# Attention stage of a one-core kernel: order of tiles, turns of q, place of the x writes, fillers and chores

## The chip, the cores and the metric

The kernel runs on one core of a Trainium2 chip. The metric is the device time in microseconds (us) of one execution, median over runs. TensorE (PE) multiplies, VectorE (DVE) and ScalarE (ACT) read its results from PSUM, GpSimd (POOL) works on SBUF only, and SyncE (SP) issues most of the transfers (DMA).

## What is computed

An attention block without softmax, and behind it a layer of eight experts with balanced routing:

```python
kv = np.einsum('bhsd,bhse->bhde', k, v)          # 8 batches, 8 heads, 576 rows, 64 wide
out = np.einsum('bhsd,bhde->bhse', q, kv)
rms = np.sqrt(np.mean(out * out, axis=-1, keepdims=True) + 1e-06)
out = out / rms * g_norm
x = out.transpose(0, 2, 1, 3).reshape(4608, 512)
logits = x @ w_gate                               # 8 columns, one for each expert
# every token goes to one expert: pairs in the order of falling logits,
# an expert is closed when it has 4608 / 8 = 576 tokens
out[mask_e] = np.maximum(x[mask_e] @ w1[e], 0.0) @ w2[e]   # 512 -> 1024 -> 512
```

## The kernel before

**Stages.** Attention comes first. x, before g_norm, is written to DRAM (x_dram). Then a search on DVE and PE finds the token list of the first expert (`threshold`, `assign`, `fetch`); its tokens are gathered from x_dram by GpSimd and the experts follow one after the other, the search for the next hidden under them. The change touches attention alone (lines 88 to 565).

**A batch of attention** has two parts. `prepare(b)` (line 367) makes what the tiles of batch b need:
- `sum_kv(r)` (391): the sum over rows of k times v for a pair of heads, four pairs r = 0 to 3, 18 matmuls each, into one PSUM tile `kv_ps`. Even and odd rows land on different partitions; ACT copies the odd ones out (`odd`, 415), DVE adds (`kv`, 417), and two copies on POOL put kv into `kvx` twice, once on each half of the partitions (423).
- `turn_q(n)` (375): four transposes of q blocks through PSUM (two for n = 4), copied to `qt` by DVE for n = 1 and 2, by ACT else. There are five, n = 0 to 4; the first half of q (h = 0) is read by n = 0, 1, 2, the second half by n = 2, 3, 4.
- kv is transposed (`t_ps`, 431), copied by ACT (`kvt`, 433), multiplied with the gate weights (`w_ps`, 442), and DVE puts the result beside kv in `kvx` (444). So a tile gives out and its part of the logits in one matmul of 72 columns.

`qt_ps`, `t_ps`, `w_ps` and fillers without a place of their own share two PSUM buffers (tag `tr`).

`tiles` (453) holds the other part. `one(t, ...)` (464) is one tile of 128 rows: 16 matmuls into `o_ps` (two buffers), then on ACT the squares `sq` (two buffers) and the copy `o_sb`, then on DVE the sums `ms`. An even batch has four tiles. An odd one has a fifth, the short tile: half its rows are the last 64 of the batch before, half the last 64 of its own, so it takes 32 matmuls of half the size and reads `qt` and `kvx` of two batches. `scale` (492) turns ms into 1/rms, one square root on ACT and four steps on DVE; `logits` (500) makes the logits of the batch (`part`, `lg`) on DVE. The scaling of x is done on POOL (511) for batches that end at or before column `last_own` = 31, that is 0 to 6, and for batch 7 by ACT in 40 small steps (516) after all else of attention (`late`).

**Order.** PE, DVE, ACT and SP run their instructions in the order in which the program writes them (`manual_schedule`, 529). `prepare` is a generator: in the loop over batches (533) each tile is followed by one step of `prepare(b + 1)`. Steps: (1) sum 0, turn 0; (2) sum 1, turn 1; (3) sums 2 and 3, odd, kv, kvx; (4) turn 2, t_ps, kvt; (5) turn 3, w_ps, turn 4. In an even batch steps 4 and 5 come without a tile between them.

**Loads.** k, v and q of a batch come in halves (`load`, 82), 576 KB each, two buffers for each name and half, all from SP. `paced` makes each DMA of SP wait until the third one before it has landed. Batches 0 and 1 are asked for at the start, the others two batches ahead, by `again` in `prepare`, in the order k v, k v, q, q.

**Writes.** Two tiles of x make one write (520). After each batch, writes go out while eight or more are waiting (`LAG` = 4), in SP's order, so in between the loads. `xo` has `LAG` + 1 = 5 buffers.

**Fillers.** `ones` (356) are matmuls of 128x512 ones in bf16 that compute nothing that is used: 18 at the start, 5 in the first preparation, two before the sums of each further one, and in each batch one before tile 0 and two before tile 3.

**Chores.** Small pieces of work that are popped from a list: first the constants for the search, then the choice of the best expert for columns 0 to 8, 9 to 17, 18 to 26 (`early`, in batches 2, 4, 6; four pieces each: cap and maximum; `pick`; `code_mx`; `best` and `over_c`). They run after each tile of batches 0 and 1, after tile 3 of each batch, in batch 6 also after tile 2, and after the logits: one, in batch 6 two.

The functions that the change touches, with the profile's line numbers:

## Time and profile before

| what | us |
|---|---|
| median of 3 runs (lowest, highest) | 659.36 (658.04, 663.68) |
| profiled execution | 660.36 |
| its span, first to last instruction | 658.6 |
| attention, first tile to the square root of batch 7 | 18.76 to 122.89 |
| first matmul of the search with all its data | 127.94 |
| first gather of tokens | 155.78 |
| busy over the span: PE, DVE, ACT, POOL | 605.8, 387.8, 194.5, 389.3 |
| mean granted TensorE clock | 0.968 of full |

The profile is of one execution. Its rows give start and duration of instructions by engine, "PEld" being weight loads of TensorE; `L479` is line 479 of the kernel; `[2.98 <-ACT o_sb L486]` says that the engine idled 2.98 us until that instruction let it go on. Busy times of overlapping instructions are longer than the distance of their starts, so distances of starts are used for a step's cost. The granted clock is the share of full speed that TensorE was given.

### The profile page before, as it was taken

What the parts mean: (1) busy time and instruction counts of PE and PEld (TensorE: products, weight loads), DVE (VectorE), ACT (ScalarE), POOL (GpSimd) and SP (SyncE); (2) the same over time, 40 slices, a digit from 0 to 9 for tenths busy, and PEclk for the clock granted to TensorE, in tenths of its full rate; (3) what the DMA queues carried; (4) which work ended last, traced back from release to release, by engine and by line L of the source; (5) the groups of instructions that cost most, each with busy time, mean ns of one, the idle gap of its engine ahead of it and who ended that gap; (6) DMA issues with size and microseconds to landing.
All of it is one profiled execution on the core that took longest, in us unless ns stands there. A gap on an engine that the chain in (4) does not pass through costs nothing.

```text
span 658.6 us, 12759 instructions
## 1 busy us (share of the span) xinstructions
PE 605.8 (92%) x4932; PEld 464.6 (71%) x4932; DVE 387.8 (59%) x1249; ACT 194.5 (30%) x395; POOL 389.3 (59%) x405
## 2 busy tenths in 40 slices
PE   7989998335899999999999999999999999999994
PEld 4767777232678677867786786778678867877873
DVE  4466667778678588668757956976671053123201
ACT  1555665611131223123212222231223123222300
POOL 1035434104585487749846974887388669848822
PEclk9999999657999999999999999999999999999998
DMA  8999989416306402710442072109103620721001
GB/s 270 310 315 295 292 291 340 154 50 199 128 0 204 164 33 71 257 41 33 158 171 73 1 262 99 41 0 323 46 32 100 229 72 1 279 84 37 0 9 64
DMA packets 49852, 91.02 MB, mean 138 GB/s; under 512 B 3712, under 2 KB 20096, under 8 KB 49792
## 3 DMA queue, kind: packets, MB, share of 16 engines
q1 hardware_dynamic: 43200, 71.31, 31.6%
q0 software_dynamic: 5888, 18.88, 8.3%
q8 instruction: 39, 0.64, 0.4%
q14 instruction: 21, 0.17, 0.1%
q10 hardware_dynamic: 704, 0.02, 0.1%
HBM read 71.32 MB, written 18.87 MB: 137 GB/s over the span
## 4 chain that ended last, share of the span: by engine, by line
PE 77%; DVE 9%; DMA 5%; issue 4%; ACT 3%; POOL 1%; POOLq 0%; SPq 0%; DVEq 0%; ACTq 0%
PE x_ps L1065 13%; PE x_ps L1025 11%; PE z_ps L1065 9%; PE y_ps L1065 9%; PE z_ps L1025 7%; PE y_ps L1025 7%; PE o_ps L479 4%; PE y_ps L1127 4%; PE kv_ps L395 3%; PE t_ps L969 3%; PE qt_ps L380 2%; DMA v_sb<-in_v_dram 2%; DMA q_sb<-in_q_dram 2%; PE given_ps L651 1%; PE given_ps L646 1%
## 5 line engine op out<-in xcount | busy, mean ns | idle before, releaser
L1070 ACT COPY h<-x_ps 128x288 f32<-128x288 f32 x93 | 37.2, 400 | 166.5 <-PE x_ps L1065 153.7
L1065 PE MATMUL x_ps<-xs,sw 128*128 128x288 f32 x248 | 71.3, 409 | 0.0
L875 POOL DMA_INDIRECT xg<-x_dram,ids x40 | 38.1, 952 | 51.8 <-DMA w_sb<-in_moe_w_dram 37.7
L992 POOL DMA_INDIRECT out_dram<-y_sb,outs x32 | 31.5, 983 | 55.8 <-DVE y_sb L1163 41.1
L1025 PE MATMUL x_ps<-tw,sh 128*128 128x256 f32 x256 | 61.6, 384 | 0.0
L972 ACT ACTIVATE xt<-t_ps,g_col 128x512 f32<-128x512 f32 (+1 forms) x40 | 25.7, 645 | 110.9 <-PE t_ps L969 110.9
L1065 PEld LDWEIGHTS x_ps<-xs,sw 128*128 128x128 f32 x248 | 46.2, 190 | 14.3 <-issue 1.7
L955 POOL TENSOR_TENSOR sw<-w_sb 128x256 f32<-128x256 f32 x64 | 46.8, 731 | 12.3 <-PE z_ps L1065 9.6
L1017 POOL TENSOR_TENSOR sh<-hid 128x512 f32<-128x512 f32 x32 | 40.7, 1272 | 19.9 <-ACT hid L1040 19.9
L1025 PEld LDWEIGHTS x_ps<-tw,sh 128*128 128x128 f32 x256 | 46.9, 190 | 7.1 <-issue 0.8
L1040 ACT ACTIVATE hid<-hid 128x576 f32<-128x576 f32 x64 | 43.8, 686 | 22.9 <-DVE hid L1079 13.1
L511 POOL TENSOR_TENSOR xo<-o_sb,inv 128x512 f32<-128x512 f32 x31 | 32.9, 1090 | 29.7 <-DVE inv L498 16.6
L1103 POOL TENSOR_TENSOR tw<-w_sb 128x512 f32<-128x512 f32 x32 | 40.1, 1276 | 5.0 <-DMA w_sb<-in_moe_w_dram 5.0
L479 PEld LDWEIGHTS o_ps<-kvx,qt 64*128 64x128 f32 (+1 forms) x640 | 33.7, 181 | 12.0 <-issue 7.1
L479 PE MATMUL o_ps<-kvx,qt 64*128 64x72 f32 (+1 forms) x640 | 38.9, 274 | 3.4 <-ACT o_sb L486 3.4
L1065 PE MATMUL z_ps<-xt,sw 128*128 128x288 f32 x128 | 37.8, 413 | 0.1
L1065 PE MATMUL z_ps<-xs,sw 128*128 128x288 f32 x128 | 37.0, 409 | 0.0
L1065 PE MATMUL x_ps<-xt,w_sb 128*128 128x288 f32 x124 | 36.8, 414 | 0.1
L1065 PE MATMUL y_ps<-xt,w_sb 128*128 128x288 f32 x128 | 36.9, 409 | 0.0
L1065 PE MATMUL y_ps<-xs,w_sb 128*128 128x288 f32 x128 | 36.7, 408 | 0.0
L490 DVE TENSOR_REDUCE ms<-sq 128x8 f32<-128x512 f32 x36 | 24.3, 683 | 20.1 <-ACT sq L485 19.8
L423 POOL COPY kvx<-kv 64x512 f32<-64x512 f32 x16 | 9.7, 607 | 43.9 <-DVE kv L417 26.9
(278 smaller groups left out, 1332.4 us busy)
## 6 DMA issues: line engine op xcount, KB each, us to landing
w_sb<-in_moe_w_dram SPq DMA_DIRECT2D x32, 512.0 KB, 5.7
w_sb<-in_moe_w_dram SPq DMA_DIRECT2D x8, 2048.0 KB, 14.3
k_sb<-in_k_dram SPq DMA_DIRECT2D x16, 576.0 KB, 5.8
v_sb<-in_v_dram SPq DMA_DIRECT2D x16, 576.0 KB, 5.8
q_sb<-in_q_dram SPq DMA_DIRECT2D x16, 576.0 KB, 6.1
x_dram<-xo SPq DMA_DIRECT2D x16, 512.0 KB, 4.4
x_dram<-xo SPq DMA_DIRECT2D x4, 256.0 KB, 4.0
xg<-x_dram,ids POOLq DMA_INDIRECT x40, 5.4
```

The lines of the kernel that those rows point to most:

```text
L479: nc.tensor.matmul(o_ps[rows_at, rp, (2 * r2 + l) * W:(2 * r2 + l + 1) * W], lhsT=turned_q[bn][ks, l, block // 2:block // 2 + m].rearrange ...
L511: nc.gpsimd.tensor_tensor(xo[:, t], o_sb[:, t, :, 0:D], inv[:, t * H:(t + 1) * H].rearrange("p (h o) -> p h o", o=1).to_broadcast([P, H, D ...
L875: tokens = nc.gpsimd.indirect_dma_start(out=xg[0:nr], out_offset=None, in_=x_dram, in_offset=bass.IndirectOffsetOnAxis(ap=ids[0:nr, n:n + ...
L955: in_order(nc.gpsimd.tensor_tensor(o, x, y, op=op))
L992: put = nc.gpsimd.indirect_dma_start(out=out, out_offset=bass.IndirectOffsetOnAxis(ap=ids_of[t][0:nr, n:n + 1], axis=0), in_=y_sb[0:nr, :] ...
L1017: in_order(nc.gpsimd.tensor_tensor(o[:, ms], x[:, ms], y[:, ms], op=op))
L1025: nc.tensor.matmul(p_ps[:, n], lhsT=left[:, f, n * P:(n + 1) * P], rhs=right[:, f], start=first, stop=(f == FH - 1), skip_group_check=True)
L1040: nc.scalar.activation(both, both, ACT.Relu)
L1065: nc.tensor.matmul(p_ps, lhsT=lhs[:, r], rhs=rhs[:, r], start=(m in (1, 2, 4, 5) and r == 0), stop=(r == 1), skip_group_check=(m in (6, 7, ...
L1070: nc.scalar.copy(u, p_ps)
L1103: in_order(nc.gpsimd.tensor_tensor(o, x, y, op=AL.subtract))
L1127: nc.tensor.matmul(y_ps[l * nr:(l + 1) * nr], lhsT=hid[:, l * FH + f, a:a + nr], rhs=w2[:, l * FH + f, :], start=(f == 0), stop=(f == FH - 1))
```

## The change

- The loads of batch 1 come in the order k v k v q q.
- `prepare` has four steps: (1) sums 0 and 1; (2) sums 2 and 3, odd, kv, kvx, turn 0; (3) t_ps, kvt, turns 1 and 2; (4) turn 3, w_ps, turn 4. In the first preparation the turns come at 0 | 1 | 2 | 3 | 4, one place earlier. The next loads are asked for in the same steps: k v, k v, q, q.
- In odd batches the short tile comes first. `qt` and `kvx` have two buffers, not three; `xo` has six.
- Fillers: one before the first and the fourth tile of batches 0 to 2 alone; the two before the sums of each preparation stay; in the first preparation 2, 6 and 5; three before t_ps in the last.
- x of batches 0 to 4 is written after batch 4, when SP has all loads behind it, that of batch 5 after batch 5, the rest at the end. `last_own` is 27, so x of batch 6 too is scaled by ACT at the end.
- Chores come after each tile of batches 0, 1 and 6, after the second and fourth tile of the others, and after the logits of batches 0 to 3.

```diff
-    for b in range(2):
-        for h in range(2):
-            for name in "kvq":
-                load(name, b, h)
+    for b, order in enumerate(("kvqkvq", "kvkvqq")):
+        for n, name in enumerate(order):
+            load(name, b, int(name in order[:n]))
...
-        qt = att.tile([P, 2, NT, HP], FT, name="qt", tag="qt", bufs=3)
+        qt = att.tile([P, 2, NT, HP], FT, name="qt", tag="qt", bufs=2)
...
+        turns = [[0], [1], [2], [3], [4]] if b == 0 else [[], [0], [1, 2], [3], [4]]
+
+        def turn_some():
+            for n in turns.pop(0):
+                turn_q(n)
+                if n in (2, 4):
+                    again("q", n // 2 - 1)
+
         if b > 0:
             ones(2, kv_ps[:, 0, :])
-        for r in range(2):
-            sum_kv(r)
-            if r:
-                again("kv", 0)
-            turn_q(r)
-            yield
+        sum_kv(0)
+        sum_kv(1)
+        again("kv", 0)
+        if b == 0:
+            ones(2)
+        turn_some()
+        yield
+        if b == 0:
+            ones(6)
         sum_kv(2)
         sum_kv(3)
         again("kv", 1)
...
-        kvx = att.tile([P, H, W], FT, name="kvx", tag="kvx", bufs=3)
+        kvx = att.tile([P, H, W], FT, name="kvx", tag="kvx", bufs=2)
         for n in range(2):
             nc.gpsimd.tensor_copy(kvx[n * D:(n + 1) * D, :, 0:D], kv.rearrange("p r l d -> p (r l) d"))
+        turn_some()
         if b == 0:
             ones(5)
         yield
-        turn_q(2)
-        again("q", 0)
+        if b + 1 == B:
+            ones(3)
...
         nc.scalar.copy(kvt, t_ps)
+        turn_some()
         yield
-        turn_q(3)
+        turn_some()
...
-        turn_q(4)
-        again("q", 1)
+        turn_some()
...
-    last_own = GC - (R + 1) // 2
+    last_own = GC - R
...
-        xo = att.tile([P, T, H, D], FT, name="xo", tag="xo", bufs=LAG + 1)
+        xo = att.tile([P, T, H, D], FT, name="xo", tag="xo", bufs=HELD)
...
-            if own or t != T - 2:
+            if not wait:
...
-            for t in range(len(rows)):
-                one(t, copies, {0: 1, 3: 2}.get(t, 0))
+            order = range(len(rows)) if b % 2 == 0 else [len(rows) - 1] + list(range(len(rows) - 1))
+            for n, t in enumerate(order):
+                one(t, copies, 1 if b < 3 and n in (0, 3) else 0, b + 1 == B and n == len(rows) - 2)
                 next(parts, None)
-                if b < 2 or t == 3 or b == 6 and t == 2:
+                if b < 2 or b == 6 or n in (1, 3):
                     chore()
...
-            if b < B - 1:
-                chore(2 if b == 6 else 1)
-
-            while len(writes) >= 2 * LAG:
+            if b < 4:
+                chore()
+
+            while b in (B - 4, B - 3) and writes:
                 writes.pop(0)()
```

More of the change, by code (lines that the diff above doesn't have):

```diff
@@ L445, in prepare @@
         kv_of[b] = kvx
-        turn_q(4)
-        again("q", 1)
-    LAG = 4
+        turn_some()
+    HELD = 6
     writes, late = [], []
-    last_own = GC - (R + 1) // 2
+    last_own = GC - R
     def tiles(c0, rows):
@@ L462, in tiles, with one @@
         own = c0 + T <= last_own
-        def one(t, copies, fill):
+        def one(t, copies, fill, wait):
             o_ps = psa.tile([P, 2, 512], FT, name="o_ps", tag="o", bufs=2)
```

## The prediction

> **What bounds the kernel now.** I read the windows first, cut where TensorE (PE) starts the first tile of a batch. The columns are busy time of PE, weight loads, VectorE (DVE), ScalarE (ACT), GpSimd (POOL), then granted clock, DMA share and GB/s.

> ```profile
> 31.62:46.49 14.87, 12.81 (x286) 10.17 (x285) 9.58 (x42) 8.16 (x16) 5.39 (x6) 1.00 0.95 310
> 59.17:72.23 13.06, 12.65 (x285) 10.07 (x283) 8.84 (x18) 8.16 (x16) 5.40 (x6) 1.00 0.89 282
> 72.23:84.92 12.69, 12.06 (x254) 9.49 (x251) 8.85 (x18) 7.14 (x14) 6.68 (x7) 1.00 0.93 321
> 97.97:111.66 13.69, 12.13 (x253) 9.49 (x251) 10.15 (x21) 7.14 (x14) 6.58 (x7) 1.00 0.87 326
> 111.66:122.89 11.23, 6.26 (x101) 5.04 (x99) 8.66 (x15) 5.92 (x12) 4.25 (x4) 0.81 0.80 300
> ```

> See that batches 3 and 4 (second and third row) are full of PE work, that batches 1 and 6 are longer with the same work, and that batch 7 (last row) is not bound by PE. The PE waits of the whole attention stage say what the rest is:

> ```profile
> PE o_ps L479 <- ACT o_sb L486: 3.4, 2, 3.0
> PE qt_ps L380 <- DMA q_sb<-in_q_dram: 2.6, 2, 1.7
> PE qt_ps L380 <- ACT kvt L433: 2.1, 4, 0.5
> PE qt_ps L380 <- DVE kvx L444: 1.2, 3, 0.4
> ```

> Two waits for q (1.65 in batch 1, 0.94 in batch 6) and one of 3.0 us in batch 7. The timeline shows where that one starts:

> ```profile
> 115.96 2.22 DVE L335 TENSOR_TENSOR over_c<-mx,cand 128x192 bf16<-128x192 f32 x2
> 118.10 2.08 DVE L490 TENSOR_REDUCE ms<-sq 128x8 f32<-128x512 f32 x3
> 118.87 0.60 ACT L485 ACTIVATE sq<-o_ps 128x512 f32<-128x512 f32 x1 [3.51 <-DVE ms L490]
> 120.05 1.24 PE L479 MATMUL o_ps<-kvx,qt 64*64 64x72 f32 x32 [2.98 <-ACT o_sb L486]
> ```

> DVE stands in the chore of batch 6 (best and over_c, 114.94 to 118.18), so the sums ms come late, ACT has no free sq, and PE no free o_ps. What follows batch 7 (sqrt at 122.89, search from 127.94, experts) is one chain that starts when attention ends; the change only shifts it.

> **The change, part by part.** A batch runs from its first tile to the end of turn 4 of the next batch. Durations on PE, from starts in the timeline of batch 4: tile 1.05 (short one 0.67), two fillers 0.54, one 0.31, a pair of k.v sums 1.31, a turn 0.59, turn 4 0.28, t_ps 0.4, w_ps 0.6.

> *Fillers.* From batch 3 on, 0.31 + 0.54 = 0.85 a batch goes; all of it stood on PE's path, since nothing was waited for there in these rows.

> [...] The trace's 0.85 has the start of the following tile in it, and is used.

> *The moved turns.* Step 3 now has t_ps, turn 1, turn 2. The three go through two PSUM buffers, so turn 2 waits for kvt, and kvt stands in ACT's queue behind sq and copy of the tile before. In batch 4 tile 3 ended at 81.80 and

> ```profile
> 82.35 0.63 ACT L486 COPY o_sb<-o_ps 128x576 f32<-128x576 f32 x1
> 82.87 0.39 ACT L433 COPY kvt<-t_ps 128x256 f32<-128x256 f32 x1
> 83.31 0.66 PE L380 MATMUL qt_ps<-ident,q_sb 128*128 128x128 f32 x4 [0.53 <-ACT kvt L433]
> ```

> So kvt is free 1.52 after a tile's end; PE has 0.4 + 0.59 to do meanwhile and idles some 0.58. Step 3 is 1.57 + 0.59 = 2.16. In step 4, turn 4 needs the buffer of turn 3, whose copy on ACT comes after sq and copy of tile 3: start 1.09 after the tile's end, 0.59 long, so turn 4 runs from 1.73 to 2.01, with 0.54 idle. That is late next where the old waits go. Sum for an even batch without fillers: 1.05 + 0.54 + 1.31 + 1.05 + 1.31 + 0.59 + 1.05 + 2.16 + 1.05 + 2.02 = 12.13, against 12.69. An odd one adds the short tile: 12.80, against 13.06. Before, an odd batch hid kvt behind its fifth tile; this is why it wins less. Batch 2 keeps 0.6 of fillers: 12.73, against 12.68.

> *Start.* With turn 1 put between the k.v sums and t_ps, t_ps waits for DVE's copy of turn 1 (0.69, behind kv 0.68), and gw's scaling waits behind turn 2's copy. I follow this to a first tile 0.8 later. Batch 0 then takes about 13.1 against 13.28: +0.6 in all. The nearest bounds: nothing, and 1.1 (those two copies and 0.47 of gw less the covered part).

> *Batches 1 and 6.* q is asked for after the second pair of sums, 5.2 after the batch's start, not 2.6. In batch 1, q landed at 36.08; it is now needed at 37.6. Batch 1 becomes 12.80 + 0.6 = 13.4, against 14.87 (-1.5). In batch 6, q landed at 101.6, when it had been issued at 95.50, behind three x writes (81.90 to 88.69). These go after all loads now, and the issues (25 loads from 27.99 to 78.35, 2.01 each) put this q's at 78.35 + 6 x 2.01 = 90.4 and its landing, 6.1 later, at 96.5; it is needed at about 101.5. The cover is 5 us; without it up to 1.1 comes back. Batch 6 becomes 12.3 (three fillers before t_ps lie in the idle before kvt, but for 0.17), against 13.69.

> Sum to the start of batch 7: +0.6 - 1.5 + 0.05 - 0.26 - 0.56 - 0.25 - 1.4 = -3.3.

> *Batch 7.* The four chores now come one after each tile of batch 6. The last (best, over_c) runs on DVE before the square root of batch 6, and beside an idle POOL: over_c of 288 took 0.45 at 127.44, with POOL idle, and 1.30 at 75.68, beside POOL's scaling. So 0.8 and not 3.3. DVE then does scale and logits of batch 6 (2.15, as 112.56 to 114.71), and ms of the first tile ends 3.5 after the batch's start. The third sq waits for that, as there are two. From there ACT (0.49 an sq, 0.54 a copy) and two o_ps buffers give the fifth sq at 5.85 and the square root at 7.4. With the chore as dear as beside POOL it is 8.8. I take 7.6: POOL's last scaling (batch 5, five of 1.07 and the two kvx copies) ends before. Against 11.23: -3.6 (bounds -2.4 and -3.8).

> *x.* Batch 6's x is now scaled by ACT after the last choice: 72 instructions each 0.241 (40 took 124.49 to 134.13), not 40: 17.4 us from about 117.6, so to 135. The last write lands 4.0 later, 139. The gather that reads it comes at 155.78 less the gain, 149, and the expert's first weights are issued at 151.04, less the gain 144. Cover 5 us: costs nothing, and one to one beyond that. POOL loses four scalings (4.25) that nothing waits for. The kvx copies now queue behind the scaling of the batch before, to 8.9 after the batch's start; needed at 12.1. SP holds 15 pieces of writing back behind all loads; it waits for nothing else before the weights. The two-buffer qt and kvx: the short tile is the last reader of the old one and runs first, so the writers find it free.

> **Sum:** 3.3 + 3.6 = 6.9; I take off 0.6 for waits of DVE work in batches 5 and 6 that the rows cannot place (kv behind two ms and a chore has 0.24 of slack): 6.3. The profiled execution took 660.36 (span 658.6, 1.8 around it), 1.0 over the median 659.36. 659.36 - 6.3 = 653.1.

> **Rivals.**
> *B, the last batch keeps its stall.* If DVE is still late (ms behind logits), batch 7 wins nothing: gain 3.3, 656.1. For it: DVE was busy 10.15 of 13.69 in batch 6. Against: the 3.2 of chore is out of the gap.
> *C, the turns stall more.* If each preparation loses 0.6 more (turn 3 or w_ps waiting for DVE's two copies in a row), six batches lose 3.6: gain 2.7, 656.7. Against: by my count the copies end 0.5 before w_ps needs them.
> *D, they stall less.* If half of the 1.12 idle I place in each batch is covered, 6 x 0.56 = 3.4 more: 649.7. For it: both stalls are set by ACT's queue, and batch 3 ran without the wait on kvt (70.32 follows the short tile at once).
> *E, slower: the granted clock falls inside attention.* [...] The clock fell here after PE had stood only since 117.06:

> ```profile
> 118.00:119.00 1.00, 0.00 (x0) 0.81 1.01 367
> 119.00:123.00 4.00, 1.24 (x32) 0.50 0.39 149
> ```

> At half clock the short tile took 1.24, not 0.73: 1.7 times. A gain of 6.3 is eaten by 6.3/0.7 = 9 us of dense work at half clock; from there on the change loses, and two whole batches at it (25 us) would give 659.4 + 11 = 670. Against: 31.62:46.49 held 1.00 with a wait of 1.65 in it, and my longest gap is 0.6.

> [...] By the trace a late q could do it, so E is kept at a small chance.

> **How the numbers follow.** Forecast 0.55 (653.1, own range 651 to 655), B and C 0.20 together, D 0.15, E 0.10. About 1% (6.6 us, 652.8) is what a measurement of this kernel tells from no change. Half of the forecast and D lie beyond: faster 0.43; the other half, B and C: within 1% 0.47; E: slower 0.10. The range takes D and C with the 1.0 between profiled run and median: 648.5 to 658.0; it leaves out E and some of D.

> **What would show it.** Right: batches 3 to 6 of 12.1 to 12.8; two PE waits a batch, on kvt before turn 2 and on turn 3's copy before turn 4, each near 0.55; no PE wait for q; square root of batch 7 within 8 us of its first tile; search round one at about 121.5. Wrong: a clock under 1.00 before 110; PE waits on DVE in steps 2 to 4; a gather that waits for an x write.

## The result and the profile after

Over 22 runs of each kernel the median went from 662.22 us to 656.74 us (654.22 to 664.02): 0.993 of before, 95% interval 0.9902 to 0.9957, within 1%. Ratios here and below leave out runs more than 1.5% above the fastest of their kernel, and they are not the quotients of the medians. The profiled execution took 654.63 with a span of 652.7, against 660.36 and 658.6. All of that came in attention: the first search matmul with all its data starts at 121.98, not 127.94 (6.0 earlier), and from there to the end both need the same (530.8 and 530.6).

The windows of the changed kernel, cut as before where TensorE (PE) starts a batch's first tile (columns: busy PE, weight loads, DVE, ACT, POOL, then granted clock, DMA share, GB/s; batches 1, 3, 4, 6 and 7):

```profile
31.89:45.20 13.31, 11.99 (x283) 9.91 (x282) 8.73 (x39) 7.40 (x15) 5.39 (x6) 1.00 0.96 325
57.81:71.47 13.66, 12.15 (x282) 10.22 (x284) 7.42 (x17) 7.40 (x15) 5.71 (x6) 1.00 0.84 270
71.47:83.39 11.92, 10.75 (x249) 9.05 (x248) 9.04 (x19) 7.78 (x15) 6.42 (x7) 1.00 0.97 339
96.39:108.71 12.32, 11.61 (x251) 9.46 (x251) 10.30 (x23) 7.88 (x15) 6.44 (x7) 1.00 0.89 334
108.71:116.94 8.23, 6.04 (x97) 5.41 (x97) 5.37 (x12) 5.95 (x13) 0.00 (x0) 0.80 0.67 253
```

Batches 1 and 6 are 1.56 and 1.37 shorter (batch 1 by 1.45, counted from PE's own start at 31.73, since the window of before begins 0.11 earlier, at a weight load), batch 7 is 3.0 shorter, batch 3 is 0.6 longer. PE's waits in attention now:

```profile
PE qt_ps L379 <- ACT kvt L444: 3.9, 6, 0.7
PE qt_ps L379 <- DVE kvx L456: 1.9, 5, 0.4
PE kv_ps L360 <- issue: 1.1, 7, 0.2
PE o_ps L490 <- ACT o_sb L497: 0.6, 2, 0.4
```

The waits for q (2.6) and the 3.0 of batch 7 are gone; the waits of the turns grew from 3.3 to 5.8. Two more of 0.39, before turn 4 in batches 0 and 1, stand in the list under other DVE work (`cells`, `parts_abs`); with them it is 6.6. The timeline of batch 7 shows why the 3.0 went:

```profile
108.34 0.52 DVE L334 TENSOR_TENSOR over_c<-mx,cand 128x192 bf16<-128x192 f32 x2
112.34 0.60 ACT L496 ACTIVATE sq<-o_ps 128x512 f32<-128x512 f32 x1 [0.36 <-DVE ms L501]
113.52 1.83 PE L490 MATMUL o_ps<-kvx,qt 64*128 64x72 f32 x16 [0.37 <-ACT o_sb L497]
```

over_c takes 0.52, not 2.22, and starts 0.4 before batch 7; the third sq waits 0.36 for ms, not 3.51. The last tile takes 1.83 where a tile takes 1.11: the clock fell in it, at about 113.7, as narrow windows of the same kernel show.

```profile
112.00:113.00 1.00, 1.00 (x18) 0.96 (x16) 0.87 (x3) 0.66 (x2) 0.00 (x0) 1.00 1.04 377
113.00:114.00 1.00, 0.63 (x10) 0.48 (x9) 0.66 (x1) 0.97 (x2) 0.00 (x0) 0.86 1.02 383
114.00:115.00 1.00, 1.00 (x14) 1.00 (x12) 0.69 (x1) 0.00 (x0) 0.00 (x0) 0.50 0.77 285
```

### The profile page after: what moved, and what is told of

The parts are those of the page before. It is cut to its first block, busy times and chain, and to the rows that moved or that the text cites. A ratio compares the mean times of both kernels' runs of the same rounds, so it can differ in the third digit from the quotient of the medians.

```text
span 652.7 us, 12759 instructions
## 1 busy us (share of the span) xinstructions
PE 601.0 (92%) x4911; PEld 464.9 (71%) x4925; DVE 383.1 (59%) x1249; ACT 201.7 (31%) x427; POOL 384.8 (59%) x401
## 4 chain that ended last, share of the span: by engine, by line
PE 77%; DVE 9%; issue 4%; DMA 3%; ACT 3%; POOL 2%; POOLq 0%; SPq 0%; DVEq 0%; ACTq 0%
PE x_ps L1077 13%; PE x_ps L1037 11%; PE z_ps L1077 9%; PE y_ps L1077 9%; PE z_ps L1037 7%; PE y_ps L1037 7%; PE o_ps L490 5%; PE y_ps L1139 4%; PE t_ps L981 3%; PE kv_ps L394 2%; PE qt_ps L379 2%; DMA v_sb<-in_v_dram 2%; PE given_ps L663 1%; ACT sq L496 1%; DVE ms L501 1%
## 5 line engine op out<-in xcount | busy, mean ns | idle before, releaser
L522 POOL TENSOR_TENSOR xo<-o_sb,inv 128x512 f32<-128x512 f32 x27 | 28.3, 1078 | 40.1 <-DVE inv L509 40.1
L490 PE MATMUL o_ps<-kvx,qt 64*128 64x72 f32 (+1 forms) x640 | 40.2, 273 | 1.4 <-ACT o_sb L497 0.6
L490 PEld LDWEIGHTS o_ps<-kvx,qt 64*128 64x128 f32 (+1 forms) x640 | 34.8, 179 | 7.0 <-issue 5.2
L501 DVE TENSOR_REDUCE ms<-sq 128x8 f32<-128x512 f32 x36 | 24.4, 681 | 23.5 <-ACT sq L496 23.4
L1169 ACT COPY u<-x_ps 128x512 f32<-128x512 f32 x24 | 14.0, 582 | 66.7 <-PE x_ps L1037 59.6
## 6 DMA issues: line engine op xcount, KB each, us to landing
w_sb<-in_moe_w_dram SPq DMA_DIRECT2D x8, 2048.0 KB, 13.1
```

The costliest lines, as they stand in the source:

```text
L490: nc.tensor.matmul(o_ps[rows_at, rp, (2 * r2 + l) * W:(2 * r2 + l + 1) * W], lhsT=turned_q[bn][ks, l, block // 2:block // 2 + m].rearrange ...
L501: nc.vector.reduce_sum(out=ms[:, t * H:(t + 1) * H], in_=sq, axis=AXX)
L522: nc.gpsimd.tensor_tensor(xo[:, t], o_sb[:, t, :, 0:D], inv[:, t * H:(t + 1) * H].rearrange("p (h o) -> p h o", o=1).to_broadcast([P, H, D ...
```

## The experiments

The theory: the fillers and the chores carry the gain, each at its predicted price, and the moved turns pay for themselves by the q waits. The rivals: the gain comes from somewhere else (the late writes, an idle POOL), or the old fillers were needed to hold the clock. Kernels a, b3, b4, c, d and e start from the changed kernel, b1 and b2 from the one before. Times are medians with the lowest in brackets, and ratios are to runs of the kernel before that were measured beside them, with their 95% interval. Since executions scatter by some 10 us (the last section has what is known of the reason), distances in one undisturbed profile and the lowest times carry more than a median.

**a1, fillers back in every batch** (in batches 0 to 2 this adds one, before the fourth tile).

```diff
-                one(t, copies, 1 if b < 3 and n in (0, 3) else 0, ...
+                one(t, copies, {0: 1, 3: 2}.get(n, 0), ...
```

> The changed kernel with the fillers before tiles as they were (one before the first, two before the fourth tile of every batch). Theory: 0.85 us of filler a batch stand on TensorE's path in batches 3 to 6, so these four get longer by 3.4 in all, and batch 7 gives some of its 0.85 back if the clock, which fell at 113.7 in the changed kernel, holds longer: search round one at 125.0 to 126.2, not 121.98. Rival: they fall into the waits on kvt and on w_ps and cost under 1 us.

Measured: 662.6 (658.57) in 10 runs, ratio 1.0008 [0.9967, 1.0049]. The lowest time is 4.3 above that of the changed kernel, and from the square root of batch 3 to that of batch 4 it takes 11.84, not 10.83. With the fillers back the change is worth nothing that these runs can tell. The later stages of its profile can't be used: issue stopped for 1.20 us, and then the clock was at half for at least the 17 us of the second row, with all fillers in place (first the row of the timeline, then that of the windows):

```profile
93.91 0.45 PE L490 MATMUL o_ps<-kvx,qt 64*128 64x72 f32 x4 [1.20 <-issue]
```

```profile
98.00:115.00 17.00, 16.67 (x235) 13.87 (x236) 6.55 (x16) 5.95 (x12) 5.26 (x5) 0.50 0.96 362
```

**a2, x written where it was written before.**

```diff
-            while b in (B - 4, B - 3) and writes:
+            while len(writes) >= 8:
```

> The changed kernel with the x writes sent as before (after each batch while eight or more wait), so three writes stand in front of the loads of batch 7. Theory: q of batch 7 is late by some 6 us, but has 5 us and more of cover since it is asked for one step later, so TensorE's wait for q is 0 to 1 us and batch 6 stays within 1 us of 12.3. Rival: the writes held back are what took the waits for loads away: a wait for q of 2 us and more returns, and the clock may fall.

Measured: 655.83 (654.93) in 10 runs, ratio 0.9913 [0.9873, 0.9953]. No wait for q is in its profile:

```profile
PE qt_ps L379 <- ACT kvt L444: 2.6, 5, 0.6
PE qt_ps L379 <- DVE kvx L456: 1.9, 5, 0.4
PE kv_ps L394 <- issue: 1.8, 1, 1.8
```

The lowest time is 0.7 above that of the changed kernel, so the place of the writes is worth at most about that, which is what the theory left for it. The profile can't say that the moved turns alone remove the wait: in it the clock was at half from 26.5 to at least 43 (last section), the search began at 129.09, and PE came to that q some 7 us later than in an undisturbed execution.

**a3, chores back in their old places.**

```diff
-                if b < 2 or b == 6 or n in (1, 3):
+                if b < 2 or n == 3 or b == 6 and n == 2:
...
-            if b < 4:
-                chore()
+            if b < B - 1:
+                chore(2 if b == 6 else 1)
```

> The changed kernel with the chores at their old places (after the fourth tile, in batch 6 after the third and fourth, then one or two after the logits). x of batch 6 stays with ScalarE. Theory: two chores of batch 6 lie behind its logits on VectorE again, ms of batch 7 is late, and batch 7 takes 10 to 11 us to its square root, not 8.2: search round one at 124 to 125. Rival: with GpSimd idle those chores are quick (0.3 to 0.5 a piece), and batch 7 loses under 1 us.

Measured: 657.1 (656.24) in 10 runs, ratio 0.9938 [0.9898, 0.9977]; search at 123.68, 1.7 later; from the square root of batch 6 to that of batch 7 8.91 against 7.85. Batch 7 loses 1.06, at the rival's bound of 1, and the search is earlier than the theory's 124 to 125. The timeline says why it isn't more: x of batch 6 is still left to ACT, so POOL is idle and the chore is cheap although it stands behind the logits.

```profile
112.67 0.52 DVE L334 TENSOR_TENSOR over_c<-mx,cand 128x192 bf16<-128x192 f32 x2
113.88 0.60 ACT L496 ACTIVATE sq<-o_ps 128x512 f32<-128x512 f32 x1 [1.26 <-PE o_ps L490]
```

**a4, x of batch 6 back on POOL.**

```diff
-    last_own = GC - R
+    last_own = GC - (R + 1) // 2
```

> The changed kernel with x of batch 6 scaled by GpSimd during batch 7, as before. Theory: the last chore is already through when GpSimd starts, so only logits run beside it: under 0.7 us. Rival: what made batch 7 quicker is that GpSimd is idle in it, and 1.5 us or more of its 3.0 come back.

Measured: 655.33 (653.96) in 4 runs, ratio 0.9894 [0.9821, 0.9968]; the same stretch 7.51 against 7.85, and over_c still 0.52. The 0.34 lies in the last tile, which takes 1.48, not 1.83. An idle POOL is not what the moved chores need. a3 and a4 together: over_c was dear only where it ran beside POOL's scaling (two took 2.22 at 115.96 in the kernel before, and 0.52 at 112.67 in a3 and 109.56 in a4), and moving either one is enough for its price; the batch is still 1.06 longer with the chore in its old place (a3).

**b1, the kernel before with the new preparation** (its steps, turns, loads and its own fillers):

```diff
-        for r in range(2):
-            sum_kv(r)
-            if r:
-                again("kv", 0)
-            turn_q(r)
-            yield
+        sum_kv(0)
+        sum_kv(1)
+        again("kv", 0)
...
+        turns = [[0], [1], [2], [3], [4]] if b == 0 else [[], [0], [1, 2], [3], [4]]
```

> The kernel before with the preparation of the changed one alone (its four steps, the turns one step on, its fillers in the first and last preparation, the load order of batch 1); short tile last, old fillers before tiles, old chores, old writes. Theory: the two waits for q go (1.65 and 0.94), but odd batches now wait for kvt (0.62 each) where the short tile hid it, and the start costs 0.2: search round one 0.3 to 1.5 earlier than 127.94. Rival: the steps are what the change lives from, 2.5 us or more earlier.

Measured: 662.33 (660.21) in 10 runs, ratio 1.0047 [1.0022, 1.0072], so slightly slower; search at 127.94, the same as before. Both theory and rival are missed. The waits for q are gone and the waits of the turns took their place in full:

```profile
PE o_ps L491 <- ACT o_sb L498: 3.4, 2, 3.0
PE qt_ps L380 <- ACT kvt L445: 3.2, 5, 0.7
PE qt_ps L380 <- DVE kvx L457: 1.9, 5, 0.4
```

The two waits of the turns make 5.1, and with the two of 0.39 that stand under other DVE work 5.9, against 3.3 for them and 2.6 for q before. With a first square root 1.07 later (33.27, not 32.20), nothing is left of the gain.

**b2, the kernel before with the new places of the chores** (the edit of a3 the other way round).

> The kernel before with the chores at the places of the changed one alone. Theory: best and over_c of batch 6 no longer stand in front of ms of batch 7, though GpSimd still scales x of batch 6 then: batch 7 takes 8 to 9.5 us to its square root, not 11.2, and search round one is at 125.5 to 126.5. Rival: with the short tile last and GpSimd at work batch 7 stays above 10.5.

Measured: 661.3 (655.81) in 10 runs, ratio 0.9994 [0.9953, 1.0035]. From the square root of batch 6 to that of batch 7 it takes 7.21, not 10.76: 3.55, the 3.6 of the prediction. The lowest run is 2.2 below the lowest of before. The median shows none of it. In the profiled execution the clock fell twice inside attention, and 3 of the 10 runs have a mean clock of 0.960 or less.

**b3, the copy of the third tile behind kvt.** This takes away what kvt waits for in ACT's queue:

```diff
-                one(t, copies, ..., b + 1 == B and n == len(rows) - 2)
+                one(t, copies, ..., n == len(rows) - 2 if b + 1 == B else n == 2)
                 next(parts, None)
+                while b + 1 < B and copies:
+                    copies.pop(0)()
```

> The changed kernel with the copy of the third tile put behind kvt in ScalarE's queue (batches 0 to 6). Theory: kvt waits only because it stands behind that copy, so TensorE's wait on kvt (0.62 to 0.75 in each of six batches, 3.9 in all) falls under 0.2 and search round one comes 3 to 3.9 earlier, at 118 to 119. Rival: the wait passes to what is late next (VectorE's copy of turn 1, o_ps of the third tile) and under 1.5 us is gained.

Measured: the wait for kvt falls from 3.9 to 0.2 and the search starts at 118.42, 3.6 earlier: ACT's queue is the cause of that wait, as expected. But the profiled span is 655.7, and the median 654.78 (654.33) in 4 runs, ratio 0.9918 [0.9897, 0.994]. Behind the search the clock fell twice more, which the changed kernel's profile does not have (windows of b3):

```profile
153.00:156.00 3.00, 3.00 (x12) 1.81 (x11) 2.71 (x8) 1.07 (x2) 2.91 (x5) 0.50 0.31 105
168.00:172.00 4.00, 4.00 (x19) 2.76 (x19) 1.69 (x6) 0.40 (x1) 0.00 (x0) 0.57 0.00 0
```

From the search's start to the end it took 537.3, not 530.7. A gain inside attention was given back behind it, in this execution.

**c1, the short tile second, not first.**

```diff
-[len(rows) - 1] + list(range(len(rows) - 1))
+[0, len(rows) - 1] + list(range(1, len(rows) - 1))
```

> The changed kernel with the short tile second in odd batches, not first. Theory: as the first tile it ends on the last blocks of q and waits for ScalarE's copy of turn 4 (it took 1.0 to 1.1, the next tile starting, where 0.66 was seen before), so the four odd batches gain 0.3 to 0.4 each: 1.2 to 1.6 earlier. Rival: its length comes from being split in 32 and it stays: no gain, or a loss where kvx of the batch before is freed later.

Measured: 656.43 (652.54) in 10 runs, ratio 0.9936 [0.9898, 0.9973]; search at 120.62, 1.4 earlier, although issue stopped for 1.35 in batch 1. From the short tile's start to the next instruction's on PE it is 0.56 in batch 3 (61.82 to 62.38), where in the changed kernel it is 1.15 (57.81 to 58.96). From the square root of batch 4 to that of batch 5 it takes 13.52, not 14.08, so the gain in such a batch is near 0.56. About half of the 1.4 is something else: batch 7 takes 7.14 between the square roots, not 7.85, because the clock did not fall in its last tile (1.11). In e1, below, where the short tile is first and the clock held as well, it takes 7.15. That the tile, standing first, waits for ACT's copy of turn 4 is only read from the order: in batch 5 that copy ran from 83.50 to 83.87, and the tile started at 83.39.

**b4, two fillers before each of the last three tiles** of batch 7, to hold the clock there:

```diff
+                if b + 1 == B and n > 1:
+                    ones(2)
                 one(t, copies, ...
```

> The changed kernel with two fillers in front of each of the last three tiles of batch 7, in a PSUM buffer of their own, so that they run while the tile waits. Theory: the clock fell at 113.7 although TensorE was busy there for 80% of the time, because tile matmuls alone (72 columns) do not hold it; with fillers it holds, the last tile takes 1.05 and not 1.83, and search round one comes 0.3 to 0.8 earlier. Rival: it falls for the idle of the waits or by the window's place alone, and nothing is gained or 0.5 lost.

Measured: 656.77 (653.8) in 10 runs, ratio 0.9935 [0.99, 0.997]. The last tile takes 1.11 and the clock holds, but the square root comes at 116.93 and the search at 121.99, as without them:

```profile
113.00:116.00 3.00, 2.34 (x32) 1.79 (x31) 1.23 (x2) 1.56 (x4) 0.00 (x0) 1.00 0.05 14
```

So the fillers won nothing: their own time took what the half clock takes. That the half clock does cost the stage 0.7 shows in e1 below, which has no fillers there: where the changed kernel takes 8.23 from the first tile of batch 7 to the square root, e1 takes 7.52 (109.93 to 117.45), with a last tile of 1.11. Its order of instructions there is the same.

**d1, b3 and c1 together.**

> The changed kernel with both edits: the copy of the third tile behind kvt, and the short tile second. Theory: the two gains add (3.6 and 1.4 and more, as that run lost 1.35 to a stop of TensorE's issue): search round one at 116 to 117.5, and, as 530.7 us follow it in undisturbed runs, a time some 5 us under the changed kernel's. Rival: what is won before the search is given back behind it, since the clock's windows do not start with the kernel: under 2 us in the time.

Measured: 654.64 (649.95) in 6 runs, ratio 0.9883 [0.9824, 0.9941]. This is the lowest median and the lowest single time of all. It beats the kernel before; against the changed kernel the lowest time is 4.3 less, but the medians (654.64 and 656.74) are not told apart by so few runs. The search starts at 120.48, not at 116 to 117.5: two stops of issue (0.66 and 1.69) and this wait in batch 5 lie before it.

```profile
90.06 1.03 PE L379 MATMUL qt_ps<-ident,q_sb 128*128 128x128 f32 x8 [1.35 <-ACT o_sb L497]
```

The profile names the put-off copy, but that copy had ended at 89.79, 0.27 before PE went on (in batch 7 of the changed kernel PE goes on 0.05 after ACT's copy, at 113.52), and 2.4 before PE went on a packet of the queue "instruction" had started (87.70). By the last section it is more likely a third stop of issue; no run separates the two.

**d2, d1 with eight warming matmuls in the search**, against the falls seen in b3:

```diff
             lowest()
+            warm(8)
```

> The same with 8 further idle matmuls of TensorE after the first search, while it waits for the gathered tokens (2.1 us of idle there in the run before, in which the clock fell again at 151 and at 168). Theory: the clock, once risen in the 14 that stand there already, holds through the wait, and the time from search round one to the end is 530 to 531.5 in every run, so runs scatter less than without. Rival: the rise comes at a fixed window whatever stands there, and the 8 cost 1 to 2 us when they run at half clock.

Measured: 656.97 (651.62) in 6 runs, ratio 0.9891 [0.9832, 0.995]. From the search to the end its profile took 531.3, as theory has it, but the runs scatter as much as before. In this profile the falls that cost most lie earlier: the clock fell twice inside attention, after stops of 1.74 and 2.15, and the search starts at 126.92.

**e1, a third of the later loads left out**: k of batches 2 to 7 is not loaded, so the kernel computes another x; all the engines' instructions stay.

```diff
                 for name in names:
-                    load(name, b + 2, h)
+                    if name == "k":
+                        loaded[name, b + 2, h] = k_sb[h]
+                    else:
+                        load(name, b + 2, h)
```

> The changed kernel with a third of the later loads left out: k of batches 2 to 7 is not loaded, and each batch reuses the k of batch 0 or 1, so x is another one; every instruction of the engines stays. Question: where do the stops of TensorE's issue inside attention and the scatter of the times come from? Theory: small transfers that feed the engines with instructions queue behind the loads, which keep the DMA engines 0.93 to 0.97 busy up to batch 7. With a DMA share of some 0.65 no stop of 0.25 us or more between 19 and 112 us is left in the profile (of thirteen profiled executions so far two had none), the clock holds 1.00 there, and the times of 10 runs lie within 3 us of the lowest (now 10 us). The lowest time itself, 654.2, stays within 1 us, since the kernel waits for no load. Rival: the stops have another cause (the branch of code, the host, refresh): stops of 0.3 to 2 us at the same places, and times scattered over 8 to 10 us as before.

Measured: 655.23 (653.63 to 657.23) in 6 runs, ratio 0.9894 [0.9853, 0.9934]. The runs lie within 3.6 us, and none has a mean clock under 0.965, where 5 of 22 of the changed kernel have 0.960 or less. The windows and the timeline of e1:

```profile
20.00:45.00 25.00, 20.81 (x487) 17.21 (x491) 13.84 (x59) 13.88 (x27) 6.61 (x8) 1.00 0.93 301
45.00:95.00 50.00, 45.19 (x1050) 38.09 (x1056) 32.61 (x76) 29.84 (x61) 23.96 (x26) 1.00 0.66 213
```

```profile
24.90 1.03 PE L394 MATMUL kv_ps<-v_sb,k_sb 64*64 64x64 f32 x48 [0.63 <-issue]
38.20 1.16 PE L394 MATMUL kv_ps<-v_sb,k_sb 64*64 64x64 f32 x59 [0.97 <-issue]
```

The theory's "no stop from 19 to 112" missed: the first 25 us still load at a DMA share of 0.93, and there two stops stand. From 45 on, at 0.66, there is none of 0.25 or more, but with all loads six of the thirteen other profiles have none there either (before, a3, a4, b1, c1, d1). And b4, with all its loads, has no mean clock of 0.960 or less in ten runs. So e1 does not tell theory from rival.

## Why the prediction was right, and where it was wrong

The mechanism was right in the main. The time lies in the stated range, but 3.6 above the forecast and outside the forecast's own 651 to 655. It agrees to 0.1 with the figure of rival C (656.7), and that is chance: C's extra waits did not come, the base was off. That the gain fits to within 0.8 is also partly luck. The start was costed 0.4 too dear and 0.6 was taken off for waits of DVE, which covered the odd batches and batch 7, costed too cheap. Of the signs named, no wait for q, the search (121.98) and the wait on kvt came as said; of batches 3 to 6 only batch 6 lies within 12.1 to 12.8, and batch 7 took 8.23, not under 8. By the prediction's own steps:

- **The base was mis-sized.** 653.1 is 659.36 less 6.3, and 659.36 was a median of three runs. Over 22 runs before has 662.22. The gain itself, 6.3, measured 5.9 in the profiled spans, 5.5 between medians and 3.8 between the lowest times. 662.22 less 6.3 is 655.9, 0.8 from the result.
- **Fillers** (0.85 a batch): upheld in the changed kernel. a1 gives 1.01 in batch 4 and 4.3 in the lowest time. No run takes them alone out of the kernel before, so their price there is not measured.
- **The moved turns** (kvt 0.58, turn 4 0.54): kvt upheld, 0.63 in batch 4, and b3 shows the cause. The second wait is another one: turn 4 waits 0.39 for DVE's copy of w_ps, and starts at 83.03 while ACT's copy of turn 3 (82.53 to 83.14) still runs. So it must share the PSUM buffer of w_ps, not of turn 3.

```profile
79.78 0.65 PE L379 MATMUL qt_ps<-ident,q_sb 128*128 128x128 f32 x4 [0.63 <-ACT kvt L444]
83.03 0.44 PE L379 MATMUL qt_ps<-ident,q_sb 128*128 128x128 f32 x2 [0.39 <-DVE kvx L456]
```

- **Even and odd batches**: batch 4 took 11.92 (12.13 predicted), batch 2 12.61 (12.73), batch 5 13.00 (12.80), batch 3 13.66 (12.80). Odd ones are too cheap in the prediction: the short tile was costed at 0.67 wherever it stands, and first in the batch it takes 0.99, and 1.15 to the next start (c1 wins that back). In batch 3 a stop of issue of 0.34 lies in the profile as well; from the square root of batch 2 it takes 14.76, where a3 and a4, without a stop there, take 14.09.
- **Start** (+0.6): mis-sized; the first tile starts 0.22 later, and batch 0 took 0.06 less.
- **Batches 1 and 6** (13.4 and 12.3): measured 13.31 and 12.32. The last q was issued at 87.22, not 90.4, so its cover was larger. But b1 shows that this gain is no gain of the turns alone: it pays for the waits that they add, and up to batch 7 the step that makes the sum positive is the fillers.
- **Batch 7** (7.6, bounds 7.4 to 8.8): 8.23. The order of events was right. What was missing is the half clock in the last tile: in e1, where the clock held, the same stretch takes 7.52. b2 and a3 measure the chores at 3.55 (beside POOL) and 1.1 to 1.7 (with POOL idle).
- **x on ACT costs nothing**: upheld, and the cover held (timeline of the changed kernel, ACT and then SP; the last write is issued at 134.8, the weights at 145.16, 10 later):

```profile
117.17 17.28 ACT L527 ACTIVATE xo<-o_sb,inv 128x64 f32<-128x64 f32 x72
```

```profile
90.81 43.99 SPq L531 DMA_DIRECT2D x_dram<-xo  x20
145.16 2.13 SPq L840 DMA_DIRECT2D w_sb<-in_moe_w_dram  x4
```

- **B, C and D**: B fell, since batch 7 lost its stall. C fell: the turns' waits are 6.6 in all, where 6 x 1.12 = 6.7 were counted. D did not happen by itself, but b3 shows that it can be made: 3.6, where D had 3.4.
- **E** (the clock falls inside attention): it happens, with the old fillers and without them. In the four kept profiles whose mean clock is 0.961 or less the clock fell inside attention before batch 7: twice with the old fillers (a1, b2), twice without (a2, d2). By that mark it would be 5 of the 22 executions of the changed kernel (0.960 or less), 3 of 10 of a1, and 14 of 78 of the kernel before, which these numbers do not tell apart.

## What to carry to other kernels

A wait that a reordering removes is worth only what the waits it adds leave: cost the reordering alone, against the kernel before, as b1 does, or its gain is credited to the wrong part. Work of DVE that is dear beside POOL (over_c 2.22 against 0.52) belongs where POOL is idle, or POOL's work elsewhere; for its price one of the two was enough (a3, a4). Where executions scatter by more than the gain, take the base from as many runs as the result, and read the parts from distances in a profile without a disturbance.

## What the runs showed of the hardware that was not expected

**Stops of TensorE's issue end 2.2 to 2.6 us after a packet of kind "instruction" started.** Inside attention PE stopped with nothing to wait for ("issue") at the same places of the program in many kernels, for 0.3 to 2.2 us, differently in each execution. The queue of kind "instruction" fits them. The profile's queue row for the changed kernel:

```profile
q8 instruction: 39, 0.64, 0.4%
```

39 packets of 16 KB in all, for 9,836 matmuls and weight loads: 252 for each. In four kernels (a4, d1, d2, e1) two stops lie 252 to 254 matmuls and 254 to 255 weight loads apart, which is two such packets. And each stop of 0.2 or more at full clock, but for one below, ends 2.2 to 2.6 us after such a packet started. In d1 a packet lies at 35.8 (the queue rows for 35.80 to 35.90):

```profile
q1 hardware_dynamic: 17, 0.04, 115.0%
q8 instruction: 1, 0.02, 59.9%
```

```profile
38.04 1.16 PE L394 MATMUL kv_ps<-v_sb,k_sb 64*64 64x64 f32 x60 [1.69 <-issue]
```

For the stop near 24 us the starts of the packet and the length of the stop were: 21.1 to 21.8, none (b3, the changed kernel, c1, a3, b4); 22.1, 0.38 (b1); 22.2, 0.53 (a1); 22.5, 0.63 (e1); 22.6, 0.66 (d1); 23.4, 1.74 (d2); 23.5, 1.75 (a2). The later the packet, the longer the stop. One packet (a4, at 21.3) took 2.3, the others here 0.9 to 1.3, and its stop of 0.83 ended 3.7 after its start. That PE stands because its next instructions are late, and that the packets are late because they stand behind the loads, is only argued, and e1 does not settle it.

**After some of these stops the clock fell.** In a2 it fell at 26.5, while PE worked on after a stop of 1.75 us (timeline and windows of a2):

```profile
26.00 1.36 PE L394 MATMUL kv_ps<-v_sb,k_sb 64*64 64x64 f32 x48 [1.75 <-issue]
```

```profile
26.00:27.00 1.00, 1.00 (x47) 0.99 (x47) 0.00 (x0) 0.00 (x0) 0.00 (x0) 0.76 0.99 371
28.00:43.00 15.00, 14.57 (x176) 10.92 (x175) 8.10 (x34) 5.33 (x11) 3.95 (x5) 0.50 0.95 313
```

**Over the same sparse tiles the clock held in one execution and fell in another.** In batch 7 of the changed kernel PE was busy 4.55 of the 5.15 us from 108.71 to 113.86, with gaps of 0.23 and 0.37, and the clock fell at about 113.7. With six more fillers it held (b4). But in e1, without them, PE was busy 4.54 of 5.15 us in the same stretch, with gaps of 0.23 and 0.38, and it held through the last tile, as in a2 and c1. So the fillers are not shown to be what holds it (windows of the changed kernel and of e1, then the timeline of e1).

```profile
108.71:113.86 5.15, 4.55 (x86) 4.01 (x86) 4.00 (x10) 4.29 (x9) 0.00 (x0) 0.99 0.87 330
109.93:115.08 5.15, 4.54 (x87) 4.01 (x88) 4.00 (x10) 4.29 (x9) 0.00 (x0) 1.00 0.02 7
```

```profile
114.74 1.11 PE L493 MATMUL o_ps<-kvx,qt 64*128 64x72 f32 x16 [0.38 <-ACT o_sb L500]
```
